# The MLP's inner width in 11 tiles of 126 units, and its weights loaded by runs of units

## The chip, the cores and the metric

The kernel runs on one core of a Trainium2 chip. The metric is the device time of one execution in microseconds; the time before is the median of three runs. A profile is one execution recorded by the hardware profiler; lines such as L101 in it are lines of the kernel's file. Engines are named as the profile has them: PE is TensorE (matmuls; PEld is its loading of weights), DVE is VectorE, ACT is ScalarE, POOL is GpSimd, SP is SyncE, whose queue (SPq) issues nearly all DMAs here.

## The reference

The input x has 2048 tokens of 512 features. Two branches work on it, and a gate, one sigmoid per token, mixes them:

```python
g = _sigmoid((x * gate_w).sum(-1, keepdims=True))
a = _A_ref(x, A_wqkv, A_w_phi, A_wo)      # linear attention, 32 heads of 16, with a learned softmax feature map
h = jnp.einsum("bsd,df->bsf", x, w1) + b1  # B: 512 -> 1376
act = h * jnp.tanh(softplus(h))            # Mish
b = jnp.einsum("bsf,fd->bsd", act, w2)     # 1376 -> 512
return g * a + (1 - g) * b
```

The change is in branch B, the MLP with an inner width of 1376 units. The gate's weight vector rides along as one more column of w1, so that 1377 units go through the first product.

## The kernel before, in words

Every large product is made of three matmuls in a reduced 4-byte type (F32R): each operand is split into a high part (a copy by ScalarE, `hi`, `wh`, `xh`) and a low part (a subtraction by GpSimd or VectorE, `lo`, `wl`, `xl`), and high x high, high x low and low x high are summed in PSUM. Four small groups stay in plain 4-byte floats: `warm` (filler at the start), `fuse`, `kvp` and `num`, and the transpose `kvT`.

**Stage A** walks over 8 chunks of 256 tokens (c = 0 to 7). For each it makes k, v and q for two groups of 128 tokens (12 matmuls of 512 columns each: `proj`), the feature map of k (`mx`, `mn`, `d0`, `d1` on VectorE, E = exp on ScalarE, the sum `S`, its reciprocal `rS` and the scaling `ml` on VectorE), and sums k's features with v (`kv`, the tile kvp) for two chunks at a time, at the end of each odd chunk up to chunk 5. q goes to DRAM (`st`, the tile pqd) for later. PSUM has three buffers that k and q (and later `up`) take in turn, four that v takes, and one for kvp. So the second k of a chunk takes the buffer that the first q of the chunk before has left, and that buffer is free once ScalarE has copied that q out (`qe`, the tile qs).

Beside this, stage A brings in the MLP's weights. w1 and w2 come in pieces of up to 1024 columns into two raw buffers (`ldw`, two pieces a chunk): w1 in chunks 0 to 2, w2 in chunks 3 to 5. One chunk later ScalarE makes the high part (`wh`) and GpSimd the low part (`wl`); the raw buffer is then free for the next piece. The orders in which the engines get these steps are written out by hand (FIRST, EVEN, ODD, NEXT, LAST, lines 39 to 58), and `pin` keeps each engine to its order. In EVEN and ODD, ScalarE gets in each chunk xh, wh0, E0, wh1, E1, ve0, ve1 (copies of v), qe0, qe1; SP gets ldx (the x of two chunks on), ldw0, ldw1, st0, st1.

**Stage B** walks over 4 blocks of 512 tokens. For each block and each of NF = 11 tiles of the inner width, `up` makes a tile of units by 512 tokens (12 matmuls: 3 products x 4 slices of the 512 features; the weights are the stationary operand, 128 units wide, and the 512 tokens move), `mi` applies Mish with the bias b1s, `hi` and `lo` split it, and `down` multiplies it with w2 for four groups of 128 tokens (3 matmuls each; here the activations are the stationary operand, units by 128 tokens, and the 512 outputs move). The attention's second half (`lq`, `num`, `wo`) goes between them. The last block's last group takes its last two tiles in `rest`, in two halves of 256 columns. The orders are BLOCK0, BLOCK1 and BLOCK.

In the version before, the 1377 units lie in two arrays: w1a (6 tiles of 128, of which the last holds 96 units, the gate's column as its 97th and zeros) and w1b (5 tiles of 128). Every tile is 128 wide. ORDER takes the tile with the gate first, so that `gr` can read the gate's row (GROW, row 96) from the first tile. b1 comes as one DMA of 128 x 11 on GpSimd's queue (L187). A piece of w1 or w2 is one DMA of 128 rows on SP's queue (`piece`, L160).

Of the kernel before, what the change touches and what calls it, by code (L numbers as in the profile page):

```python
# [9 lines left out]
F32 = mybir.dt.float32  # L10
F32R = mybir.dt.float32r
AF = mybir.ActivationFunctionType
# [3 lines left out]
P = 128  # L16
# [4 lines left out]
KT = D // P  # L21
# [5 lines left out]
FA = 736  # L27
NFA = 6
FB = 640
NFB = 5  # L30
NF = NFA + NFB
GROW = FA % P
ORDER = [NFA - 1] + list(range(NFA - 1)) + list(range(NFA, NF))
WARM = 10


# [53 lines left out]
def tile_gated_mix(ctx: ExitStack, tc: tile.TileContext, xT, wv, wkT, wqT, bd, w1a, w1b, b1, w2a, w2b, wo, out):  # L90
# [6 lines left out]
    pin = tc.keep_in_program_order  # L97
    V, G_, A_, Sy = nc.vector, nc.gpsimd, nc.scalar, nc.sync

    def mm(*a, **k):  # L100
        return pin(nc.tensor.matmul(*a, **k))  # L101

    def T(shape, dt, tag, bufs, name):
        nm[0] += 1
        return sp.tile(shape, dt, name=f"{name}_{nm[0]}", tag=tag, bufs=bufs)
# [4 lines left out]
    def k4(name, tag, dt=F32):  # L110
        return T([P, 1024], dt, tag, {"E": 4, "tx": 2, "oh": 2, "z": 1}[tag], name)

    def k2(name, tag, dt=F32):
        return T([P, 512], dt, tag, {"pq": 3, "io": 4, "hl": 8}[tag], name)

    def psum(name, tag, bufs={"a": 3, "dn": 4, "kv": 1}):
        nm[0] += 1
        return pp.tile([P, 512], F32, name=f"{name}_{nm[0]}", tag=tag, bufs=bufs[tag])

    def act(out_, in_, fn=AF.Copy, **k):  # L120
        return pin(A_.activation(out_, in_, fn, **k))  # L121
# [7 lines left out]
    def f32(ap):  # L129
        return ap.bitcast(F32)  # L130
# [3 lines left out]


    def stage(wT):
        return T([P, NFA * 512], F32, "w1a", 2, "wT")[:, : KT * 512].rearrange("p (k g f) -> p k g f", k=KT, f=P)

    skT, sqT = stage(wkT), stage(wqT)
    bds = k2("bds", "io")[:, :].rearrange("p (g f) -> p g f", g=NG)  # L140
# [17 lines left out]
    def piece(dram, o, n=1024):  # L158
        r = k4("raw", "oh")
        pin(Sy.dma_start(r[:, :n], dram[:, o : o + n]))  # L160
        return r[:, :n]
# [22 lines left out]
    pin(G_.affine_select(md, md, pattern=[[-DH, 8], [0, DH]], compare_op=ALU.is_ge, fill=0.0, base=0, channel_multiplier=1))  # L184
    pin(G_.affine_select(md, md, pattern=[[DH, 8], [0, DH]], compare_op=ALU.is_ge, fill=0.0, base=DH - 1, channel_multiplier=-1))
    b1s = const.tile([P, NF], F32, name="b1s")
    pin(G_.dma_start(b1s, b1))  # L187
    ident = const.tile([P, P], F32, name="ident")
    make_identity(nc, ident)
    mask = const.tile([P, 2, 2, 32], F32, name="mask")  # L190
# [10 lines left out]
    def at(key, name, fn):  # L201
        steps.setdefault((key, name), []).append(fn)
# [143 lines left out]
            at(key, "ldx", lambda: ldx(c + 2))  # L346


    W = {}
    for n_, f in (("w1a", NFA), ("w1b", NFB), ("w2a", NFA), ("w2b", NFB)):  # L350
        W[n_] = None, f * 512
    raws = {}
    PIECES = [(n_, dram, o) for n_, dram in (("w1a", w1a), ("w1b", w1b), ("w2a", w2a), ("w2b", w2b)) for o in range(0, W[n_][1], 1024)]

    def w_ops(c):

        for j, (n_, dram, o) in enumerate(PIECES[2 * c : 2 * c + 2]):
            cs = slice(o, min(o + 1024, W[n_][1]))

            def ld(n_=n_, dram=dram, cs=cs):  # L360
                raws[n_, cs.start] = piece(dram, cs.start, cs.stop - cs.start)

            def wh(n_=n_, cs=cs):
                hl, n = W[n_]
                if hl is None:
                    hl = [T([P, n], F32R, n_, 2, n_ + x) for x in "hl"]
                    W[n_] = hl, n
                act(hl[0][:, cs], raws[n_, cs.start])

            def wl(n_=n_, cs=cs):  # L370
                h, l = W[n_][0]
                pin(G_.tensor_sub(l[:, cs], raws[n_, cs.start], f32(h[:, cs])))

            at(("A", c), f"ldw{j}", ld)
            at(("A", c + 1), f"wh{j}", wh)
            at(("A", c + 1), f"wl{j}", wl)

    def w1_tile(f, x, k):
        n_, f, n = ("w1a", f, NFA) if f < NFA else ("w1b", f - NFA, NFB)
        return W[n_][0][x][:, (k * n + f) * P : (k * n + f + 1) * P]  # L380

    def w2_tile(f, x):
        n_, f = ("w2a", f) if f < NFA else ("w2b", f - NFA)
        return W[n_][0][x][:, f * 512 : (f + 1) * 512]


    xb = {}
# [86 lines left out]
    def b_ops(b):  # L474
        key = ("B", b)
        U, dn, tts, eTs, num, ohl, io = {}, {}, {}, {}, {}, {}, {}

        def up(i):
            f = ORDER[i]
            xh, xl = xb[b]  # L480
            ps = psum("up", "a")
            n = 0
            for w, a in ((0, xh), (1, xh), (0, xl)):
                for k in range(KT):
                    mm(ps, w1_tile(f, w, k), a[:, k, :], start=(n == 0), stop=(n == 3 * KT - 1))
                    n += 1
            U[i] = {"ps": ps}

        def mi(i):
            f = ORDER[i]  # L490
            U[i]["a"] = k2("act", "hl")
            act(U[i]["a"], U[i]["ps"], AF.Mish, bias=b1s[:, f : f + 1])

        def hi(i):
            U[i]["h"] = k2("h", "hl", F32R)
            act(U[i]["h"], U[i]["a"])

        def lo(i):
            U[i]["l"] = k2("l", "hl", F32R)
            pin(G_.tensor_sub(U[i]["l"], U[i]["a"], f32(U[i]["h"])))  # L500

        last_t = 3 if b == NB - 1 else None

        def down(i, t):
            if t not in dn:
                dn[t] = psum("down", "dn")
            f = ORDER[i]
            h, l = [U[i][x][:, t * P : (t + 1) * P] for x in "hl"]
            for n, (a, x) in enumerate(((h, 0), (h, 1), (l, 0))):
                mm(dn[t], a, w2_tile(f, x), start=(i == 0 and n == 0), stop=(i == (NF - 3 if t == last_t else NF - 1) and n == 2))  # L510

        for i in range(NF):
            at(key, f"up{i}", lambda i=i: up(i))
# [3 lines left out]
            for t in range(4):  # L517
                if t != last_t or i < NF - 2:
                    at(key, f"dn{i}" if i < NF - (2 if b == NB - 1 else 1) else f"df{t}", lambda i=i, t=t: down(i, t))


        cs = slice(4 * b, 4 * b + 4)
# [95 lines left out]
        for t in range(4):  # L618
            def wo_(t=t):
                num["wo", t] = ps = psum("wo", ("kv", "a")[t % 2])  # L620
                woh, wol = [kt(wob[x], 512) for x in "hl"]
                n = 0
                for G in range(NG):
                    o = (G % 2) * SC + (t % 2) * P
                    hl = ohl[t // 2, G // 2]
                    h, l = hl[:, o : o + P], hl[:, 512 + o : 512 + o + P]
                    for a, w in ((h, woh), (h, wol), (l, woh)):
                        mm(ps, a, w[:, G, :], start=(n == 0), stop=(n == 3 * NG - 1))
                        n += 1

            def ag(t=t):
                i = 4 * b + t
                io[t] = k2("io", "io")
                act(io[t], num["wo", t], scale=g_sb[:, i : i + 1])

            def most():

                i = S // P - 1
                pin(V.scalar_tensor_tensor(io[3], dn[3], og_sb[:, i : i + 1], io[3], op0=ALU.mult, op1=ALU.add))

            def rest():

                i = S // P - 1
                for j, eng in enumerate((Sy, A_)):
                    cs = slice(256 * j, 256 * j + 256)
                    ps = psum("rest", "a")[:, :256]
                    n = 0
                    for u in (NF - 2, NF - 1):
                        h, l = [U[u][x][:, 3 * P :] for x in "hl"]
                        for a, x in ((h, 0), (h, 1), (l, 0)):  # L650
                            mm(ps, a, w2_tile(ORDER[u], x)[:, cs], start=(n == 0), stop=(n == 5))
                            n += 1
                    pin(V.scalar_tensor_tensor(io[3][:, cs], ps, og_sb[:, i : i + 1], io[3][:, cs], op0=ALU.mult, op1=ALU.add))  # L653
                    pin(eng.dma_start(out[i * P : (i + 1) * P, cs], io[3][:, cs]))

            def fi(t=t):
                i = 4 * b + t
                pin(V.scalar_tensor_tensor(io[t], dn[t], og_sb[:, i : i + 1], io[t], op0=ALU.mult, op1=ALU.add))
                pin(Sy.dma_start(out[i * P : (i + 1) * P, :], io[t]))

            at(key, f"wo{t}", wo_)
            at(key, f"ag{t}", ag)
            if t == last_t:
# [51 lines left out]
    for j in range(2):  # L715
        h, l = [w[:, 2 * j : 2 * j + 2, :].rearrange("p k f -> p (k f)") for w in (wvh, wvl)]
# [14 lines left out]
    for i in range(4):  # L731
        wh, wl = [halves(w, slice(i // 2 * 2, i // 2 * 2 + 2))[i % 2] for w in (wqh, wql)]
# [77 lines left out]
```

## Time and profile before

| what | value |
|---|---|
| median of 3 runs | 451.03 us (450.79 to 451.19) |
| profiled execution | 451.0 us |
| its span, first to last instruction | 449.3 us |
| instructions in it | 7222 |
| TensorE clock granted, mean | 0.999 |
| DMA | 40.09 MB, mean 89 GB/s |

The profile's parts are the busy time of each engine as a share of the span, the chain of work that ended last (followed back from the last instruction, each step to what released it), groups of equal instructions with their mean time, and the DMA queues. A row of a timeline or chain begins with its start and its length in us; a group of n instructions in a row ends in xn. A window of the DMA view lists packets by size.

### The profile page before, as it was taken

How to read it: one execution, taken by the hardware profiler on the slowest of the kernel's cores; microseconds unless marked ns; L12 is line 12 of the kernel's file. 1: busy time of each engine (PE TensorE's matmuls, PEld its weight loads, DVE VectorE, ACT ScalarE, POOL GpSimd, SP SyncE). 2: the span in 40 equal slices, each digit the busy share in tenths (PEclk: the TensorE clock that was granted, in tenths of full speed). 3: DMA queues.
4: the chain of work that ended last, by engine and by line, in shares of the span. 5: the costliest groups of instructions: out<-in, count | busy, mean ns of one | idle time of the engine just before them, and what ended most of it. 6: DMA issues, size and time to landing. Idle time of an engine off the chain costs nothing.

```text
span 449.3 us, 7222 instructions
## 1 busy us (share of the span) xinstructions
PE 443.9 (99%) x2886; PEld 362.8 (81%) x2886; DVE 306.0 (68%) x408; ACT 195.0 (43%) x269; POOL 163.0 (36%) x102
## 2 busy tenths in 40 slices
PE   8999999999999999999999999999999999999997
PEld 7888888888888888878787887887887888787885
DVE  2798558459399999997979976476967529611003
ACT  3644533444325555627355453534253543244221
POOL 3448687677862345621122212014212122221211
PEclk9999999999999999999999999999999999999999
DMA  7721522514523111405143151331151302030002
GB/s 272 268 95 47 190 69 95 190 15 172 189 84 106 48 24 25 117 19 154 64 125 111 39 148 48 82 107 47 36 149 47 86 13 95 1 82 13 1 0 95
DMA packets 25883, 40.09 MB, mean 89 GB/s; under 512 B 5749, under 2 KB 14197, under 8 KB 25849
## 3 DMA queue, kind: packets, MB, share of 16 engines
q1 hardware_dynamic: 25528, 39.22, 28.6%
q8 instruction: 23, 0.38, 0.3%
q10 hardware_dynamic: 288, 0.39, 0.3%
q14 instruction: 12, 0.09, 0.1%
q0 software_dynamic: 32, 0.01, 0.0%
HBM read 22.82 MB, written 8.40 MB: 69 GB/s over the span
## 4 chain that ended last, share of the span: by engine, by line
PE 98%; DMA 1%; ACT 0%; DVE 0%; issue 0%
PE proj L101 29%; PE up L101 27%; PE down L101 26%; PE wo L101 10%; PE num L101 2%; PE kvp L101 2%; DMA bds<-in_bd_dram 1%; PE fuse L101 1%; PE rest L101 0%; PE z L101 0%; ACT wkh L121 0%; PE warm L101 0%; DVE io L653 0%; PE kvT L456 0%
## 5 line engine op out<-in xcount | busy, mean ns | idle before, releaser
L500 POOL TENSOR_TENSOR l<-act,h 128x512 fp32r<-128x512 f32 x44 | 63.2, 1438 | 221.9 <-ACT h L121 183.6
L121 ACT ACTIVATE act<-up,b1s 128x512 f32<-128x512 f32 x44 | 30.3, 688 | 89.0 <-PE up L101 88.8
L320 POOL TENSOR_TENSOR zacc<-zacc,E 128x1024 f32<-128x1024 f32 x16 | 39.7, 2483 | 42.7 <-DVE E L282 32.6
L121 ACT ACTIVATE E<-E 128x1024 f32<-128x1024 f32 x32 | 33.6, 1059 | 47.3 <-DVE E L267 44.3
L282 DVE TENSOR_TENSOR E<-E,Sm 128x1024 f32<-128x1024 f32 x32 | 45.7, 1427 | 1.1
L271 DVE TENSOR_REDUCE Sm<-E 128x64 f32<-128x1024 f32 x32 | 38.7, 1210 | 5.0 <-ACT E L121 5.0
L101 PE MATMUL wo<-woh,ohl 128*128 128x512 f32 x128 | 40.7, 389 | 0.0
L101 PE MATMUL down<-w2ah,h 128*128 128x512 f32 x96 | 37.5, 390 | 0.0
L101 PE MATMUL down<-w2al,h 128*128 128x512 f32 x96 | 37.4, 390 | 0.0
L101 PE MATMUL down<-w2ah,l 128*128 128x512 f32 x96 | 37.4, 389 | 0.0
L258 DVE TENSOR_REDUCE mx<-proj 128x32 f32<-128x512 f32 x16 | 11.0, 690 | 30.7 <-PE proj L101 30.7
L101 PE MATMUL down<-w2bh,h 128*128 128x512 f32 x78 | 30.5, 391 | 0.0
L101 PE MATMUL down<-w2bl,h 128*128 128x512 f32 x78 | 30.4, 390 | 0.0
L101 PE MATMUL down<-w2bh,l 128*128 128x512 f32 x78 | 30.4, 389 | 0.0
L121 ACT ACT_TABLE_LOAD x19 | 24.4, 1283 | 10.1 <-PE up L101 9.8
L121 ACT ACTIVATE h<-act 128x512 fp32r<-128x512 f32 x44 | 27.8, 632 | 1.4
L612 DVE TENSOR_TENSOR ohl<-num,ohl 128x512 fp32r<-128x512 f32 x16 | 10.3, 683 | 26.5 <-ACT ohl L121 26.3
L101 PEld LDWEIGHTS wo<-woh,ohl 128*128 128x128 f32 x128 | 24.0, 188 | 5.0
L101 PE MATMUL up<-xbh,w1ah 128*128 128x512 f32 x96 | 26.2, 395 | 0.0
L101 PE MATMUL up<-xbh,w1al 128*128 128x512 f32 x96 | 25.7, 390 | 0.0
L101 PE MATMUL up<-xbl,w1ah 128*128 128x512 f32 x96 | 25.7, 390 | 0.0
L405 DVE TENSOR_TENSOR xbl<-xraw,xbh 128x1024 fp32r<-128x1024 f32 x8 | 12.2, 1562 | 19.8 <-ACT xbh L121 19.8
(121 smaller groups left out, 966.6 us busy)
## 6 DMA issues: line engine op xcount, KB each, us to landing
eT<-tt SPq DMA_DIRECT2D x128, 64.0 KB, 2.0
xraw<-in_xT_dram SPq DMA_DIRECT2D x15, 512.0 KB, 4.4
pqd<-qs SPq DMA_DIRECT2D x16, 256.0 KB, 3.1
pq<-pqd SPq DMA_DIRECT2D x16, 256.0 KB, 2.9
out_dram<-io SPq DMA_DIRECT2D x15, 256.0 KB, 2.1
raw<-in_w1a_dram SPq DMA_DIRECT2D x3, 512.0 KB, 4.3
raw<-in_w2a_dram SPq DMA_DIRECT2D x3, 512.0 KB, 4.0
wT<-in_wkT_dram SPq DMA_DIRECT2D x4, 256.0 KB, 5.2
```

The lines of the kernel that those rows point to most:

```text
L101: return pin(nc.tensor.matmul(*a, **k))
L121: return pin(A_.activation(out_, in_, fn, **k))
L258: pin(V.tensor_reduce(d[name], hv(src()), axis=AX.X, op=op))
L271: pin(V.tensor_reduce(d["S"], hv(d["E"][:, :]), axis=AX.X, op=ALU.add))
L282: pin(eng.tensor_mul(hv(d["E"][:, :]), hv(d["E"][:, :]), d["S"][:, :, None].to_broadcast([P, 2 * H, DH])))
L320: at(key, f"z{t}", lambda d=d: pin(G_.tensor_add(zacc, zacc, d["E"])))
L405: pin(V.tensor_sub(xb[b][1][:, :, sl], kt(raw[h], SC), f32(xb[b][0][:, :, sl])))
L500: pin(G_.tensor_sub(U[i]["l"], U[i]["a"], f32(U[i]["h"])))
L612: pin(V.tensor_sub(ohl[h, gp][:, 512:], num[h, gp], f32(ohl[h, gp][:, :512])))
```

## The change

The 1377 units are put in one row: first the 97 of the tile with the gate, then w1a's first 640, then w1b's 640 (RUNS). This row is cut into 11 tiles of 126 units, the last of 117. `size(i)` is the width of tile i, and `runs(o, n)` says which stretches of the arrays in DRAM units o to o + n are. The arrays in DRAM are as before.

- w1 becomes one pair of arrays of 4 x 1377 columns in SBUF (before: two pairs, with 4 x 768 and 4 x 640). Its pieces are six, as before, and each is filled by one to four DMAs of 128 rows, one for each run of columns, 17 in all.
- A tile of w2 now holds rows of up to two stretches of DRAM that lie on other partitions than in SBUF. Each stretch is loaded by one DMA of so many rows of 2 KB, 21 in all, and its units' b1 by another DMA of as many rows of one element, on the same queue. The numbers of rows by tile are: 97 and 29; 99 and 27; 101 and 25; 103 and 23; 105 and 21; 107 and 19; 109 and 17; 111 and 15; 113 and 13; 115 and 11; 117. The pieces are as before, two tiles each, the last with one.
- `up` has weights of 126 (117) columns, `mi`, `hi`, `lo`, `wh` and `wl` of w2 work on 126 (117) partitions, and `down` and `rest` multiply over 126 (117) rows.
- The orders by hand, the number of matmuls and their order are as before; ORDER goes, since the tile with the gate comes first in the row.

```diff
-NF = NFA + NFB
-GROW = FA % P
-ORDER = [NFA - 1] + list(range(NFA - 1)) + list(range(NFA, NF))
+RUNS = (("a", 640, FA - 640 + 1), ("a", 0, 640), ("b", 0, FB))
+GROW = FA - 640
+NU = FA + 1 + FB
+FT = 126
+NF = -(-NU // FT)
...
-    pin(G_.dma_start(b1s, b1))
...
+    def runs(o, n):
+        r, z = [], 0
+        for part, u, m in RUNS:
+            a, e = max(o, z), min(o + n, z + m)
+            if a < e:
+                r.append((part, u + a - z, e - a, a - o))
+            z += m
+        return r
+
+    def size(i):
+        return min(FT, NU - i * FT)
+
+    W = {"w1": (None, KT * NU), "w2a": (None, NFA * 512), "w2b": (None, NFB * 512)}
...
+    def ld_w1(r, o, n):
+        for k in range(KT):
+            a, e = max(o, k * NU), min(o + n, (k + 1) * NU)
+            for part, u, m, z in runs(a - k * NU, e - a) if a < e else ():
+                src, f = (w1a, NFA * P) if part == "a" else (w1b, FB)
+                pin(Sy.dma_start(r[:, a - o + z : a - o + z + m], src[:, k * f + u : k * f + u + m]))
+
+    def ld_w2(r, i):
+        for part, u, m, z in runs(i * FT, size(i)):
+            while m:
+                j, p = divmod(u, P)
+                c = min(m, P - p)
+                pin(Sy.dma_start(r[z : z + c, :], (w2a if part == "a" else w2b)[p : p + c, j * 512 : (j + 1) * 512]))
+                j += 0 if part == "a" else NFA
+                pin(Sy.dma_start(b1s[z : z + c, i : i + 1], b1[p : p + c, j : j + 1]))
+                u, m, z = u + c, m - c, z + c
...
-            def ld(n_=n_, dram=dram, cs=cs):
-                raws[n_, cs.start] = piece(dram, cs.start, cs.stop - cs.start)
+            def ld(n_=n_, o=o, n=n, tiles=tiles):
+                raws[n_, o] = k4("raw", "oh")
+                if n_ == "w1":
+                    ld_w1(raws[n_, o], o, n)
+                for i, z in tiles:
+                    ld_w2(raws[n_, o][:, z : z + 512], i)
...
-                act(hl[0][:, cs], raws[n_, cs.start])
+                act(hl[0][:rows, cs], raws[n_, cs.start][:rows, :n])
...
-                pin(G_.tensor_sub(l[:, cs], raws[n_, cs.start], f32(h[:, cs])))
+                pin(G_.tensor_sub(l[:rows, cs], raws[n_, cs.start][:rows, :n], f32(h[:rows, cs])))
...
-    def w1_tile(f, x, k):
-        n_, f, n = ("w1a", f, NFA) if f < NFA else ("w1b", f - NFA, NFB)
-        return W[n_][0][x][:, (k * n + f) * P : (k * n + f + 1) * P]
+    def w1_tile(i, x, k):
+        o = k * NU + i * FT
+        return W["w1"][0][x][:, o : o + size(i)]
...
-            ps = psum("up", "a")
+            ps = psum("up", "a")[: size(i), :]
...
-            act(U[i]["a"], U[i]["ps"], AF.Mish, bias=b1s[:, f : f + 1])
+            act(U[i]["a"], U[i]["ps"], AF.Mish, bias=b1s[: size(i), i : i + 1])
```

More of the change, by code (lines that the diff above doesn't have):

```diff
@@ L136, in stage @@
     def stage(wT):
-        return T([P, NFA * 512], F32, "w1a", 2, "wT")[:, : KT * 512].rearrange("p (k g f) -> p k g f", k=KT, f=P)
+        return T([P, KT * NU], F32, "w1", 2, "wT")[:, : KT * 512].rearrange("p (k g f) -> p k g f", k=KT, f=P)
     skT, sqT = stage(wkT), stage(wqT)
@@ L346, in a_ops @@
             at(key, "ldx", lambda: ldx(c + 2))
-    W = {}
-    for n_, f in (("w1a", NFA), ("w1b", NFB), ("w2a", NFA), ("w2b", NFB)):
-        W[n_] = None, f * 512
-    raws = {}
-    PIECES = [(n_, dram, o) for n_, dram in (("w1a", w1a), ("w1b", w1b), ("w2a", w2a), ("w2b", w2b)) for o in range(0, W[n_][1], 1024)]
+    def runs(o, n):
[6 more added lines that the diff above has]
+        return r
@@ new lines, in size @@
+    def size(i):
+        return min(FT, NU - i * FT)
+    W = {"w1": (None, KT * NU), "w2a": (None, NFA * 512), "w2b": (None, NFB * 512)}
+    raws = {}
+    PIECES = [(n_, o) for n_, (_, f) in W.items() for o in range(0, f, 1024)]
+    def ld_w1(r, o, n):
[4 more added lines that the diff above has]
+                pin(Sy.dma_start(r[:, a - o + z : a - o + z + m], src[:, k * f + u : k * f + u + m]))
@@ L355, in w_ops @@
+    def ld_w2(r, i):
[7 more added lines that the diff above has]
+                u, m, z = u + c, m - c, z + c
     def w_ops(c):
-        for j, (n_, dram, o) in enumerate(PIECES[2 * c : 2 * c + 2]):
+        for j, (n_, o) in enumerate(PIECES[2 * c : 2 * c + 2]):
@@ L358, in w_ops @@
             cs = slice(o, min(o + 1024, W[n_][1]))
-            def ld(n_=n_, dram=dram, cs=cs):
-                raws[n_, cs.start] = piece(dram, cs.start, cs.stop - cs.start)
-            def wh(n_=n_, cs=cs):
-                hl, n = W[n_]
+            n = cs.stop - o
+            tiles = [] if n_ == "w1" else [(o // 512 + (NFA if n_ == "w2b" else 0) + t, t * 512) for t in range(n // 512)]
+            rows = min([size(i) for i, _ in tiles], default=P)
+            def ld(n_=n_, o=o, n=n, tiles=tiles):
[4 more added lines that the diff above has]
+                    ld_w2(raws[n_, o][:, z : z + 512], i)
@@ L365, in wh, with wl @@
+            def wh(n_=n_, cs=cs, n=n, rows=rows):
+                hl, m = W[n_]
                 if hl is None:
-                    hl = [T([P, n], F32R, n_, 2, n_ + x) for x in "hl"]
-                    W[n_] = hl, n
-                act(hl[0][:, cs], raws[n_, cs.start])
-            def wl(n_=n_, cs=cs):
+                    hl = [T([P, m], F32R, n_, 2, n_ + x) for x in "hl"]
+                    W[n_] = hl, m
+                act(hl[0][:rows, cs], raws[n_, cs.start][:rows, :n])
+            def wl(n_=n_, cs=cs, n=n, rows=rows):
@@ L376, in w_ops, with w2_tile @@
             at(("A", c + 1), f"wl{j}", wl)
-    def w1_tile(f, x, k):
-        n_, f, n = ("w1a", f, NFA) if f < NFA else ("w1b", f - NFA, NFB)
-        return W[n_][0][x][:, (k * n + f) * P : (k * n + f + 1) * P]
-    def w2_tile(f, x):
-        n_, f = ("w2a", f) if f < NFA else ("w2b", f - NFA)
-        return W[n_][0][x][:, f * 512 : (f + 1) * 512]
+    def w1_tile(i, x, k):
+        o = k * NU + i * FT
+        return W["w1"][0][x][:, o : o + size(i)]
+    def w2_tile(i, x):
+        n_, j = ("w2a", i) if i < NFA else ("w2b", i - NFA)
+        return W[n_][0][x][: size(i), j * 512 : (j + 1) * 512]
     xb = {}
@@ L478, in up @@
         def up(i):
-            f = ORDER[i]
             xh, xl = xb[b]
-            ps = psum("up", "a")
+            ps = psum("up", "a")[: size(i), :]
             n = 0
@@ L484, in up @@
                 for k in range(KT):
-                    mm(ps, w1_tile(f, w, k), a[:, k, :], start=(n == 0), stop=(n == 3 * KT - 1))
+                    mm(ps, w1_tile(i, w, k), a[:, k, :], start=(n == 0), stop=(n == 3 * KT - 1))
                     n += 1
@@ L489, in mi @@
         def mi(i):
-            f = ORDER[i]
-            U[i]["a"] = k2("act", "hl")
-            act(U[i]["a"], U[i]["ps"], AF.Mish, bias=b1s[:, f : f + 1])
+            U[i]["a"] = k2("act", "hl")[: size(i), :]
+            act(U[i]["a"], U[i]["ps"], AF.Mish, bias=b1s[: size(i), i : i + 1])
         def hi(i):
-            U[i]["h"] = k2("h", "hl", F32R)
+            U[i]["h"] = k2("h", "hl", F32R)[: size(i), :]
             act(U[i]["h"], U[i]["a"])
         def lo(i):
-            U[i]["l"] = k2("l", "hl", F32R)
+            U[i]["l"] = k2("l", "hl", F32R)[: size(i), :]
             pin(G_.tensor_sub(U[i]["l"], U[i]["a"], f32(U[i]["h"])))
@@ L506, in down @@
                 dn[t] = psum("down", "dn")
-            f = ORDER[i]
             h, l = [U[i][x][:, t * P : (t + 1) * P] for x in "hl"]
             for n, (a, x) in enumerate(((h, 0), (h, 1), (l, 0))):
-                mm(dn[t], a, w2_tile(f, x), start=(i == 0 and n == 0), stop=(i == (NF - 3 if t == last_t else NF - 1) and n == 2))
+                mm(dn[t], a, w2_tile(i, x), start=(i == 0 and n == 0), stop=(i == (NF - 3 if t == last_t else NF - 1) and n == 2))
         for i in range(NF):
@@ L650, in rest @@
                         for a, x in ((h, 0), (h, 1), (l, 0)):
-                            mm(ps, a, w2_tile(ORDER[u], x)[:, cs], start=(n == 0), stop=(n == 5))
+                            mm(ps, a, w2_tile(u, x)[:, cs], start=(n == 0), stop=(n == 5))
                             n += 1
```

## The prediction, made before the changed kernel ran

> **What bounds the kernel now.** I read the page first: its busy shares, then the chain of work that ended last.
>
> ```profile
> span 449.3 us, 7222 instructions
> PE 443.9 (99%) x2886; PEld 362.8 (81%) x2886; DVE 306.0 (68%) x408; ACT 195.0 (43%) x269; POOL 163.0 (36%) x102
> PE 98%; DMA 1%; ACT 0%; DVE 0%; issue 0%
> ```
>
> TensorE's matmuls are busy 99% of the span and make 98% of the chain: no other engine, queue or transfer is late anywhere now, so only what makes a matmul longer, or makes one wait, changes the time. The profiled execution took 451.0 us, 1.7 us more than its span; the median of the three runs is 451.03 us, so sums made on the profiled one carry over as they stand.
>
> The chain in order of time gives the price of single matmuls (columns: start us, us, engine, group, matmuls):
>
> ```profile
> 6.71 0.64 PE warm L101 x4
> ...
> 114.39 1.92 PE kvp L101 x128
> ...
> 163.47 2.72 PE up L101 x12
> 166.19 0.44 PE kvT L456 x4
> ...
> 444.58 1.44 PE rest L101 x12
> ```
>
> up: 12 matmuls moving 512 columns in 2.72 us, 226.7 ns each. rest: same kind, 256 columns, 1.44/12 = 120.0 ns. The slope is 106.7/256 = 0.4167 ns a column, so 512 columns cost 213.3 ns and 13.3 ns are left over whatever the width: the part of the weight load that shows. 13.3 ns is 32 column times for 128 weight columns, four at a time. In the two plain 4-byte groups much more shows: kvT, 128 columns through a 128-column load, takes 110 ns, 56.7 above its 53.3; warm takes 160 ns, which is three times 53.3, two for moving and one for the load. There a load goes one column at a time.
>
> **Part 1: narrower weight tiles in up.** The order on TensorE is the same, 2886 matmuls. down and rest keep 128 weight columns (the tokens) and have 126 or 117 rows in them. up's weight tile has 126 columns (117 in the last of 11 tiles). The cost of such a load is in no row. From below: 13.3 ns, the nearest row by type; a saving is excluded but for 2/128 of it. From above: kvT's 56.7 ns times 126/128, 55.8. I take the upper kind, because 13.3 ns is a quarter of 128 columns and 126 has no four equal quarters, and price it at the array's own pace: 126 x 0.4167 = 52.5 ns, for 117 columns 48.8. up runs 4 blocks x 11 tiles x 12 = 528 matmuls, 480 wide and 48 narrow: 480 x 39.2 + 48 x 35.4 ns = **20.5 us** (22.2 at kvT's price), all on the path, since up's matmuls stand in the chain back to back. A tile of 12 goes from 2.72 to 3.19 us.
>
> The Trainium skill ("TensorE: Matmul & The Clock Gate", "Weight-path perf modes — Fast Weight Load (FWL) and DoubleRow") says that the fast load is on when the number of weights is 128 and the type isn't FP32. By it the sum stands as I have it. The same page ("LDWEIGHTS (loading the stationary operand)") gives columns / 1.2 ns; by that an estimate is 105 ns a load, and the sum would be 48 us.
>
> **Part 2: w2 and b1 in runs of units.** A piece of w2 was one DMA of 128 rows; now each of its tiles is one or two runs of units, and each run two DMAs on SP's queue: rows of 2 KB and a column of b1, 4 bytes a row. SP's queue grows by 47 instructions. How many transfer engines does such a DMA use? Each engine ends its share with a small packet, so packets under 512 B count engines. Three windows: one piece of w2a, 128 rows (71.0 to 75.2 us, whose 40 slices also show when bytes begin, 71.9); the single row gd<-gr (158.6 to 159.9); and pq, rows of 2 KB at full load (162.1 to 162.6).
>
> ```profile
> GB/s 0 0 0 0 0 0 0 0 0 156 195 195 78 195 351 312 273 273 273 234 312 351 546 390 273 390 78 39 78 0 0 0 0 0 0 0 0 0 0 0
> DMA packets 144, 0.52 MB, mean 125 GB/s; under 512 B 16, under 2 KB 16, under 8 KB 144
> ```
> ```profile
> DMA packets 2, 0.00 MB, mean 2 GB/s; under 512 B 1, under 2 KB 1, under 8 KB 2
> ```
> ```profile
> DMA packets 92, 0.19 MB, mean 373 GB/s; under 512 B 1, under 2 KB 1, under 8 KB 92
> ...
> q1 hardware_dynamic: 92, 0.19, 98.0%
> ```
>
> 128 rows went to 16 engines in equal shares, one row to one. Runs here have 97, 101, 103, 107, 109, 113 rows: primes, which have no equal shares but one. The bounds: 16 engines (no cost: as many bytes as before) or one. I take equal shares, on the same first engines each time, the pattern of both rows. In the third window, 0.5 us, 16 engines x 0.5 x 98% = 7.84 us of engine time carried 91 rows: 86 ns a row of 2 KB on one engine. The 4-byte element is priced by ge_sb<-gd, 512 of them (160.9 to 161.8):
>
> ```profile
> DMA packets 535, 0.02 MB, mean 18 GB/s; under 512 B 528, under 2 KB 528, under 8 KB 535
> ```
>
> That window is 0.9 us long, 32 elements an engine: at most 28 ns each, at least nothing beside other work. Halfway, 14, makes 100 ns a row, bounds 86 and 114. With shares by the largest divisor up to 16, the first engine gets these rows of each piece: A (tiles 0, 1) 97+29+9+3 = 138; B (2, 3) 101+5+103+23 = 232; C (4, 5) 7+3+107+19 = 136; D (6, 7) 109+17+37+1 = 164; E (8, 9) 113+1+23+1 = 138; F 9. B alone is 23.2 us of one engine, and a stage-A chunk is 16.4 us.
>
> The Trainium skill ("DMA: Bandwidth & Descriptors", "Why a DMA increments its semaphore by 16 and not by 1") says that a DMA takes the largest number up to 16 dividing its slowest dimension, the lowest-numbered engines on SP's queue, and one engine for 127 partitions. No run here shows that yet; by it the sum stands.
>
> Who waits? ScalarE converts each piece in order, ahead of E, v and qs of the same chunk. Rows of SP, ScalarE, GpSimd, VectorE and TensorE, in that order:
>
> ```profile
> 71.07 8.30 SPq L160 DMA_DIRECT2D raw<-in_w2a_dram  x2
> ```
> ```profile
> 81.22 1.05 ACT L121 ACTIVATE w2ah<-raw 128x1024 fp32r<-128x1024 f32 x1
> 87.10 1.06 ACT L121 ACTIVATE E<-E 128x1024 f32<-128x1024 f32 x1 [4.83 <-DVE E L267]
> 88.07 1.04 ACT L121 ACTIVATE w2ah<-raw 128x1024 fp32r<-128x1024 f32 x1
> 89.83 1.06 ACT L121 ACTIVATE E<-E 128x1024 f32<-128x1024 f32 x1 [0.71 <-DVE E L267]
> 90.79 0.58 ACT L121 ACTIVATE v<-proj 128x512 f32<-128x512 f32 x1
> 92.67 0.60 ACT L121 ACTIVATE v<-proj 128x512 f32<-128x512 f32 x1 [1.29 <-PE proj L101]
> 95.44 0.60 ACT L121 ACTIVATE qs<-proj 128x512 f32<-128x512 f32 x1 [2.17 <-PE proj L101]
> ```
> ```profile
> 103.42 2.43 POOL L372 TENSOR_TENSOR w2al<-raw,w2ah 128x1024 fp32r<-128x1024 f32 x1
> ```
> ```profile
> 108.92 1.21 DVE L271 TENSOR_REDUCE Sm<-E 128x64 f32<-128x1024 f32 x1
> 110.17 0.55 DVE L279 RECIPROCAL Sm<-Sm 128x64 f32<-128x64 f32 x1
> 110.76 1.90 DVE L282 TENSOR_TENSOR E<-E,Sm 128x1024 f32<-128x1024 f32 x1
> ```
> ```profile
> 100.63 1.07 PE L101 MATMUL proj<-wkh,xh 128*128 128x512 f32 x4
> ...
> 135.41 1.07 PE L101 MATMUL proj<-wkh,xh 128*128 128x512 f32 x4
> ```
>
> A is issued at 71.07 and moves from 72.0 to 85.8 (before, to 74.0 by the slices); its conversion slips from 81.2 to 86, which E at 87.10 still covers: nothing. B ends at 109.0, and its conversion, due at 88.07, ends at 110.0; behind it E, two v and the first qs end at 112.9. The second k of chunk 5 needs the PSUM buffer of that qs: it starts at 112.9 instead of 100.63. C follows two stores of qs and the next x, 2.7 us of each engine (64 KB of each engine's share at 373/16 GB/s):
>
> ```profile
> xraw<-in_xT_dram SPq DMA_DIRECT2D x15, 512.0 KB, 4.4
> pqd<-qs SPq DMA_DIRECT2D x16, 256.0 KB, 3.1
> ```
>
> C runs from 111.7 to 125.3, D to 141.7 (GpSimd has freed its buffers in time: B's low part, 2.43 us, ends by 114). D's conversion, E and the three VectorE steps add 5.8: chunk 5's kv can start at 147.5. TensorE has run out of other work at 127.5 (112.9 + 5 groups of 2.72 + chunk 4's kv) and waits 20 us. kv of chunk 5 is the second half of the kvp row, due at 115.35: **32.1 us** late. In one line: 72.0 + 670 rows x 100 ns + 2.7 + 5.8 - 115.35; with 86 ns it is 22.8, with 114 ns 41.5. E lands at 158.2 and its followers on ScalarE free their PSUM buffer by 164; TensorE wants it for chunk 7's second k, at 135.41 + 32.1 = 167.5, so nothing is added, and F is 9 rows.
>
> **Part 3: the restart.** After the idle start TensorE was slow for a while:
>
> ```profile
> 1.12 4.21 PE L101 MATMUL warm<-ones 128*128 128x128 f32 x20 [1.12 <-DVE ones L170]
> ```
>
> 20 matmuls took 4.21 us that take 3.2 at warm's later pace: 1.0 us lost. Two long waits: **2.0 us**, between 0 and 4.
>
> **Parts at nothing.** w1 as one array: 17 DMAs of 128 rows for 6, all in equal shares of 16. At SP's 0.33 us each they delay a piece by at most 1.0 us:
>
> ```profile
> 38.46 0.33 SPq L160 DMA_DIRECT2D raw<-in_w1a_dram  x1
> ```
> ```profile
> 46.44 1.05 ACT L121 ACTIVATE w1ah<-raw 128x1024 fp32r<-128x1024 f32 x1
> ```
> ```profile
> raw<-in_w1a_dram SPq DMA_DIRECT2D x3, 512.0 KB, 4.3
> ```
>
> It lands at 42.8 and is used at 46.44: 3.7 us cover it; without the cover it costs 1 us. Mish, h and l work on 126 partitions with the same 512 elements each, beside TensorE. b1's old DMA on POOL goes from a queue that nobody waits for. What is late next, after part 1, is TensorE itself.
>
> **Sum:** 451.0 + 20.5 + 32.1 + 2.0 = **505.6 us**; within this case 494 (451.0 + 20.5 + 22.8) to 519 (451.0 + 22.2 + 41.5 + 4).
>
> **Rivals.** (1) Only the transfers cost: the load of 126 columns keeps its 13.3 ns, or a longer one hides behind the 213 ns of the matmul ahead. For it: the load unit's 81% is below the matmuls' 99%. Against: 13.3 ns shows in every row of this type, and full loads in kvT and warm. 451.0 + 34.1 = 485.1. The same page of the Trainium skill ("Step-by-step: what each phase is for") says that loads are pulled ahead of matmuls in flight; by that it would be this case. (2) Only the loads cost: uneven runs are dealt over 16 engines, or each onto another engine. Then the longest run, 115 rows, is 11.5 us, and a piece has 17 us from issue (71.07) to use (88.07). 471.5. (3) down loses too, because its weights have 126 rows: 522 + 12 loads x 40 ns (53.3 - 13.3) = 21.4 more: 527.0. (4) Not slower: load and shares both stay as in the rows of before; TensorE moves the same columns in the same order, and the narrower load saves at most 0.2 ns x 528 = 0.1 us. It decides where a 126-column load shows under 14 ns and no run of w2 takes over 17 us. 451.0.
>
> **Chances.** Forecast 0.62, (1) 0.14, (2) 0.13, (3) 0.05, (4) 0.06. The range leaves out (3) and (4) and has to take in (2): 471 to 519. A measurement of this kernel tells about 0.2% from no change. Case (4) gives same 0.05 and faster 0.01; slower by over 0.2% gets 0.94.
>
> **What would show it.** up x12 at 3.19 us in the chain with down still at 2.72 (part 1; 2.72 refutes it, down at 3.2 is rival 3). raw<-in_w2a landing after 10 us or more, ScalarE's w2 conversions waiting for DMA, TensorE idle some 12 us before the second k of chunk 5 and some 20 us before its kv (part 2; landings near 4 us refute it). w1 pieces landing near 4 us (covered). I am most easily wrong in the 4-byte elements' price and in the chain of waits behind B and D.

## The result, and the profile after

The changed kernel took **482.69 us** (median of 5 runs, 482.06 to 483.12) against 451.03 us before (5 runs, 450.79 to 451.19): 1.0702 times as long, 95% interval 1.0689 to 1.0715. It is slower, inside the predicted range, but 23 us faster than the forecast of 505.6. The time is closest to rival (1), "only the transfers cost", at 485.1. The profiled execution took 483.1 us.

The page of the changed kernel, its busy shares, two rows of its 40 slices and its chain:

```profile
span 481.4 us, 7299 instructions
PE 453.3 (94%) x2886; PEld 365.2 (76%) x2886; DVE 304.6 (63%) x408; ACT 194.1 (40%) x269; POOL 160.9 (33%) x101
PE   8999999939439999999999999999999999999997
PEclk9999999988859999999999999999999999999999
PE 76%; SPq 12%; DVE 6%; DMA 2%; issue 2%; POOL 1%; ACT 1%; POOLq 0%; ACTq 0%
```

TensorE was busy all along before; now it has a hole in the slices that run from about 96 to 144 us, the granted clock (PEclk) sags there, and SP's queue stands in the chain with 12%. From about 150 us on all is full again. So I split the time at the first up, which ends stage A. First the rows before the change (the first is the first k of chunk 6, used further down), then the one after:

```profile
116.24 1.20 PE L101 MATMUL proj<-wkh,xh 128*128 128x512 f32 x4
...
151.39 1.20 PE L101 MATMUL up<-xbh,w1ah 128*128 128x512 f32 x4
```
```profile
179.45 1.19 PE L104 MATMUL up<-xbh,w1h 128*126 128x512 f32 x4
```

Stage A grew by 28.1 us. The rest of the span was 449.3 - 151.4 = 297.9 and is 481.4 - 179.5 = 301.9: stage B grew by 4.0. Together 32.1, the growth of the span.

**Where stage A lost it.** ScalarE's timeline in the changed kernel, its conversions of the pieces B, C and D of w2, with the idle time ahead of each and what ended it:

```profile
105.93 1.06 ACT L124 ACTIVATE w2ah<-raw 126x1024 fp32r<-126x1024 f32 x1 [17.55 <-DMA raw<-in_w2a_dram]
106.89 1.04 ACT L124 ACTIVATE E<-E 128x1024 f32<-128x1024 f32 x1
120.51 1.06 ACT L124 ACTIVATE w2ah<-raw 126x1024 fp32r<-126x1024 f32 x1 [9.47 <-DMA raw<-in_w2b_dram]
121.47 1.04 ACT L124 ACTIVATE E<-E 128x1024 f32<-128x1024 f32 x1
136.11 1.06 ACT L124 ACTIVATE w2bh<-raw 126x1024 fp32r<-126x1024 f32 x1 [13.59 <-DMA raw<-in_w2b_dram]
137.07 1.04 ACT L124 ACTIVATE E<-E 128x1024 f32<-128x1024 f32 x1
```

TensorE's timeline beside it: the second k of chunk 5 waits for a qs, and the kv of chunk 5 for v and E, all of which stand behind those conversions on ScalarE:

```profile
109.45 2.07 PE L104 MATMUL proj<-wkh,xh 128*128 128x512 f32 x4 [8.44 <-ACT qs L124]
111.32 1.57 PE L104 MATMUL proj<-wkl,xh 128*128 128x512 f32 x4
112.72 1.07 PE L104 MATMUL proj<-wkh,xl 128*128 128x512 f32 x4
...
138.65 1.08 PE L104 MATMUL kvp<-E,v 128*32 128x64 f32 x32 [12.95 <-ACT v L124]
141.35 1.08 PE L104 MATMUL kvp<-E,v 128*32 128x64 f32 x32 [1.62 <-DVE E L284]
142.37 2.08 PE L104 MATMUL proj<-wkh,xh 128*128 128x512 f32 x4
144.24 1.91 PE L104 MATMUL proj<-wkl,xh 128*128 128x512 f32 x4
145.95 1.35 PE L104 MATMUL proj<-wkh,xl 128*128 128x512 f32 x4
147.14 1.08 PE L104 MATMUL proj<-wkh,xh 128*128 128x512 f32 x4
```

These are the two waits of the prediction, at the same two instructions and by the same chain, each somewhat shorter. The first row after each wait also shows the slow restart: a group of four takes 2.07 us where it settles at 1.07. The granted clock goes with it: it was 0.50 from 138.6 to 146.0 us, 0.88 from 146.0 to 148.1 and 1.00 from there to the end of stage A.

**How many engines carried a run?** Two windows of the DMA view, 88 to 104 us and 110 to 130 us, in which nearly only runs of w2 and b1 move:

```profile
GB/s 26 26 26 26 26 20 26 26 26 41 87 51 16 1 21 21 26 5 26 26 26 26 26 26 26 26 26 26 26 26 26 26 20 26 26 26 26 1 11 26
DMA packets 440, 0.40 MB, mean 25 GB/s; under 512 B 243, under 2 KB 243, under 8 KB 440
...
q1 hardware_dynamic: 440, 0.40, 7.5%
```
```profile
DMA packets 482, 0.48 MB, mean 24 GB/s; under 512 B 254, under 2 KB 254, under 8 KB 481
...
q1 hardware_dynamic: 481, 0.47, 6.9%
```

The shares are taken over 16 engines, so one busy engine is 1/16 = 6.25%: 7.5 and 6.9% say that there was little more than one at work, at 26 GB/s in most slices, where the 128-row piece of before had reached 546. The small packets can't count engines here, since most of them are b1's elements; the share can.

**Stage B**, first a down of the kernel before (its up stands in the prediction, 2.72), then the chain of the changed kernel:

```profile
160.75 2.72 PE down L101 x12
```
```profile
186.69 2.79 PE up L104 x12
189.47 2.74 PE down L104 x12
```

up went from 2.72 to 2.79 us, not to the predicted 3.19. down is at 2.74. Each has about 44 such groups of 12 (4 blocks x 11 tiles): 44 x 0.07 = 3.1 us for up and 44 x 0.02 = 0.9 us for down make the 4.0.

### The profile page after: what moved, and what is told of

Same layout as the page of the kernel before. It is cut to its first block, busy times and chain, and to the rows that moved or that the text cites. A ratio compares the mean times of both kernels' runs of the same rounds, so it can differ in the third digit from the quotient of the medians.

```text
span 481.4 us, 7299 instructions
## 1 busy us (share of the span) xinstructions
PE 453.3 (94%) x2886; PEld 365.2 (76%) x2886; DVE 304.6 (63%) x408; ACT 194.1 (40%) x269; POOL 160.9 (33%) x101
## 4 chain that ended last, share of the span: by engine, by line
PE 76%; SPq 12%; DVE 6%; DMA 2%; issue 2%; POOL 1%; ACT 1%; POOLq 0%; ACTq 0%
PE up L104 25%; PE down L104 25%; PE proj L104 12%; PE wo L104 9%; SPq L381 8%; SPq L383 4%; PE num L104 2%; DVE Sm L273 1%; DMA pqd<-qs 1%; DVE E L284 1%; DMA bds<-in_bd_dram 1%; DVE xbl L444 1%; PE fuse L104 1%; DVE E L269 1%; PE kvp L104 1%
## 5 line engine op out<-in xcount | busy, mean ns | idle before, releaser
L537 POOL TENSOR_TENSOR l<-act,h 126x512 fp32r<-126x512 f32 (+1 forms) x44 | 63.9, 1453 | 223.6 <-ACT h L124 153.8
L104 PE MATMUL up<-xbh,w1h 128*126 128x512 f32 (+1 forms) x176 | 48.7, 398 | 0.0
L104 PE MATMUL up<-xbl,w1h 128*126 128x512 f32 (+1 forms) x176 | 48.1, 395 | 0.2 <-DVE xbl L444 0.2
L104 PE MATMUL up<-xbh,w1l 128*126 128x512 f32 (+1 forms) x176 | 48.0, 394 | 0.0
L104 PEld LDWEIGHTS up<-xbh,w1h 128*126 128x126 f32 (+1 forms) x176 | 32.1, 186 | 10.1 <-issue 2.9
L104 PEld LDWEIGHTS up<-xbl,w1h 128*126 128x126 f32 (+1 forms) x176 | 32.6, 186 | 8.9 <-DVE xbl L444 0.6
L104 PEld LDWEIGHTS up<-xbh,w1l 128*126 128x126 f32 (+1 forms) x176 | 32.6, 185 | 8.1
L104 PE MATMUL down<-w2ah,h 126*128 126x512 f32 x96 | 37.6, 391 | 0.0
L104 PE MATMUL down<-w2ah,l 126*128 126x512 f32 x96 | 37.5, 391 | 0.0
L104 PE MATMUL down<-w2al,h 126*128 126x512 f32 x96 | 37.5, 391 | 0.0
```

## The experiments

The theory after the result: a DMA whose number of rows has no divisor but one goes to a single engine, and this is the whole of stage A's 28 us; a 126-column load costs little, since it hides beside the matmul ahead. Runs told as one time were single executions with a profile.

**1. The kernel before, its w2 in runs of 97 and 31 rows** (two primes). Nothing else is changed:

```diff
-                raws[n_, cs.start] = piece(dram, cs.start, cs.stop - cs.start)
...
+                for o in range(0, cs.stop - cs.start, 512):
+                    for p0, p1 in ((0, 97), (97, P)):
+                        pin(Sy.dma_start(r[p0:p1, o : o + 512], dram[p0:p1, cs.start + o : cs.start + o + 512]))
...
```

> The kernel before, tiles of 128 units, but each tile of w2 is loaded by two DMAs, of 97 and of 31 rows of 2 KB (before: one DMA of 128 rows for two tiles). Nothing else changes. Theory (a number of rows that no number up to 16 divides goes to one engine, the same each time): all 256 rows of a piece pass one engine at 86 to 91 ns, 22 to 23 us a piece against chunks of 16.4 us; by the prediction's sum the kv of chunk 5 is 72.0 + 1024 rows x 88 ns + 2.7 + 5.8 - 115.35 = 55 us late, and the next piece adds some 5, restarts some 5: 516 us, 505 to 525. Rival (uneven runs are dealt over all engines, or each to another engine): 451 to 453 us, landings near 4 us.

Measured: 515.37 us (before, beside it: 451.13, 13 runs). ScalarE's waits in it (us in all, times, longest):

```profile
ACT w2ah L121 <- DMA raw<-in_w2a_dram: 49.2, 3, 18.9
ACT w2bh L121 <- DMA raw<-in_w2b_dram: 36.9, 2, 18.8
```

Full 128-unit tiles, no b1 in between, the same bytes: 64 us lost by the row counts alone.

**2. The same with runs of 96 and 32 rows.** The edit is that of run 1 with 96 for 97.

> The same as e1_before_97_31 with runs of 96 and 32 rows: as many DMAs and bytes. Theory (equal shares on 16 engines): 451.0 us, within 0.5, up at 2.72 us a tile. Rival (the cost is in the number of DMAs or in SP's issuing): as slow as with 97 and 31 rows, over 470 us.

Measured: 451.63 us (451.27 to 451.92, 10 runs), 1.0011 times before, interval 1.0002 to 1.0021. The same number of DMAs and one row of difference: half a microsecond. Its DMA view in the window of 71 to 76 us, where four DMAs were issued:

```profile
DMA packets 320, 0.52 MB, mean 105 GB/s; under 512 B 64, under 2 KB 64, under 8 KB 320
...
q1 hardware_dynamic: 320, 0.52, 35.8%
```

64 small packets from four DMAs are 16 engines each, counted as the prediction counted them. So neither the splitting nor SP's longer queue costs more than that; the row counts do. The Trainium skill's rule in "DMA: Bandwidth & Descriptors" ("Why a DMA increments its semaphore by 16 and not by 1"), the largest number up to 16 that divides the rows, agrees with runs 1 and 2 and with the 6.9% above.

**3. The changed kernel with w2 and b1 laid out by tiles in DRAM**, so that each piece is one DMA of 128 rows again; the 126-unit tiles and w1 stay:

```diff
+    pin(G_.dma_start(b1s, b1))
...
-                for i, z in tiles:
-                    ld_w2(raws[n_, o][:, z : z + 512], i)
+                else:
+                    pin(Sy.dma_start(raws[n_, o][:, :n], (w2a if n_ == "w2a" else w2b)[:, o : o + n]))
...
```

> The changed kernel with w2 and b1 laid out in DRAM in its own order of units, so that a piece of w2 is one DMA of 128 rows again and b1 one DMA of 128 x 11 on POOL's queue. up's tiles of 126 and w1's runs stay. Theory (the wait in stage A comes from w2's and b1's runs alone; the rest is up's tiles at 2.79 us for 2.72): 451.0 + 44 x 0.07 + at most 1 = 453.5 to 455.5 us, no wait of TensorE in stage A. Rival (w1's narrow runs or something else of the new layout make the wait): 470 us or more.

Measured: 455.33 us (455.18 to 455.44), 1.0093 times before, 1.0078 to 1.0108. In its timeline the first up starts where it does in the kernel before; in its chain up is as slow as in the changed kernel:

```profile
151.40 1.19 PE L104 MATMUL up<-xbh,w1h 128*126 128x512 f32 x4
```
```profile
158.15 2.79 PE up L104 x12
```

So the loads of w2 and b1 are all of stage A's loss (w1's 17 DMAs cost nothing), and what is left, some 4 us, comes with the new tiles, which are narrower and start at other columns.

**4. The changed kernel with b1 as one DMA on GpSimd's queue again**, laid out by tiles in DRAM, and w2's runs as they are, to part the rows from the 4-byte elements:

```diff
+    pin(G_.dma_start(b1s, b1))
...
-                pin(Sy.dma_start(b1s[z : z + c, i : i + 1], b1[p : p + c, j : j + 1]))
...
```

> The changed kernel with b1 as one DMA of 128 x 11 on POOL's queue again (b1 laid out by tiles in DRAM), so that SP's queue loses the 21 DMAs of single elements; w2's runs stay. Theory A (an element costs about 5 ns on its engine, as the landings of the changed kernel give: 91 ns a row of data and element less 86 for the data): 670 x 5 = 3.5 us less than the changed kernel, 479 us, 476 to 482. Theory B (an element costs 28 ns, ge_sb's pace): 19 us less, 464 us.

Measured: 478.57 us (478.26 to 479.06), 1.0612 times before, 1.0594 to 1.0629. b1's 21 DMAs cost 4.1 of the 28 us; over the 670 elements ahead of the second wait that is 6 ns each, not 14, if all of it goes by the element and none by the DMA. The rows of w2 are the rest. Without b1 the small packets count engines again: in the window of 71 to 84.5 us, in which piece A passes, 22 packets are under 512 B. The runs of A have 97, 29, 99 and 27 rows, and 1 + 1 + 11 + 9 is 22, the equal shares that the prediction counted with.

**5. The price of a narrower load: the kernel before, with up's tiles narrowed in place** to 128, 127, 126, 125, 124, 120, 112, 117, 96, 126 and 128 columns by step. The units cut off are left out of the sum.

```diff
-        return W[n_][0][x][:, (k * n + f) * P : (k * n + f + 1) * P]
+        return W[n_][0][x][:, (k * n + f) * P : (k * n + f) * P + wid]
...
```

> The kernel before with up's weight tiles narrowed in place, at their old start addresses: widths by step 0 to 10 of a block 128, 127, 126, 125, 124, 120, 112, 117, 96, 126, 128 columns; Mish, h, l and the rows of w2 narrow with them, so the units that are cut off are left out of the sum. One look at up's matmuls by width. Theory A (the 5 to 6 ns more of a matmul in the changed kernel come from a load that isn't 128 columns wide): the narrowed steps take 2.78 to 2.80 us, the two of 128 take 2.72. Theory B (they come from where the columns start in SBUF): every step takes 2.72 us, 451 us in all. The prediction's price of a load of single columns, 2.9 us or more for some width, would show only where a width falls out of the fast form.

**6. The kernel before, with up's 128 columns starting 0, 1, 2, 3, 4, 8, 16, 32, 1, 2 and 0 columns further right** by step. The products are then those of the wrong units.

```diff
-        return W[n_][0][x][:, (k * n + f) * P : (k * n + f + 1) * P]
+        return W[n_][0][x][:, (k * n + f) * P + off : (k * n + f + 1) * P + off]
...
```

> The kernel before with up's weight tiles 128 columns wide, but starting 0, 1, 2, 3, 4, 8, 16, 32, 1, 2, 0 columns (of 4 bytes) to the right for steps 0 to 10 of a block, so that shifted steps multiply by the wrong columns. Theory A (width): every step 2.72 us, 451 us in all. Theory B (start address): the steps with offsets that aren't a multiple of 16 columns take 2.78 to 2.80 us, the others 2.72; 453 us in all.

Measured: 454.14 and 453.55 us (before, beside them: 451.0, 7 runs). From the traces, the mean time from one matmul's start to the next inside a tile, without the first two of a tile, in ns, step by step:

```
step               0      1      2      3      4      5      6      7      8      9     10
5: width         128    127    126    125    124    120    112    117     96    126    128
5: ns          226.9  226.7  233.4  231.7  228.3  233.0  230.4  235.8  229.9  233.3  227.9
6: start +         0      1      2      3      4      8     16     32      1      2      0
6: ns          227.0  231.8  230.4  229.2  226.6  233.4  233.4  232.8  232.2  230.8  226.7
```

A width of 126 costs 6.5 ns a matmul, and none costs near the 39.2 of the prediction. 127 columns, with no equal quarters either, cost nothing, which leaves nothing of the quarters. But the small loss isn't one of width alone: 128 columns from another start lose as much, and +4 loses nothing where +8 does. A width or a start that stands in two steps gives the same within 1 ns, so this is hardly noise, though each kernel ran once. Neither theory had it, and **its cause stays open**.

**7. The changed kernel with each run split at its largest multiple of 16**, b1 as one DMA, w2's place in DRAM unchanged:

```diff
-                pin(Sy.dma_start(r[z : z + c, :], (w2a if part == "a" else w2b)[p : p + c, j * 512 : (j + 1) * 512]))
+                for q0, q1 in ((0, c // 16 * 16), (c // 16 * 16, c)):
+                    if q0 < q1:
+                        pin(Sy.dma_start(r[z + q0 : z + q1, :], (w2a if part == "a" else w2b)[p + q0 : p + q1, j * 512 : (j + 1) * 512]))
...
```

> The changed kernel with b1 as one DMA on POOL's queue, and each run of w2 split in two DMAs: the largest multiple of 16 rows, and the rest of under 16 rows. DRAM's w2 stays as it was. Theory (16 equal shares, and a rest of n rows goes to n engines): a piece lands about as fast as before; TensorE doesn't wait in stage A, or under 2 us at SP's 16 issues a piece; 451.0 + 4.3 for up = 455.3 us, 454.5 to 458. Rival (each DMA of the piece has its own price on the way, whatever its rows): with twice as many DMAs as in the kernel with b1 apart, over 478 us.

Measured: 454.70 us (454.38 to 455.03), 1.0079 times before, 1.0062 to 1.0096. More DMAs, and the wait is gone. ScalarE's conversions of A and B in its timeline are back at their old places (81.22 and 88.07 before):

```profile
81.35 1.05 ACT L124 ACTIVATE w2ah<-raw 126x1024 fp32r<-126x1024 f32 x1
88.19 1.04 ACT L124 ACTIVATE w2ah<-raw 126x1024 fp32r<-126x1024 f32 x1
```

Its DMA view in the window of 71 to 76 us, in which the eight DMAs of piece A move:

```profile
DMA packets 345, 0.52 MB, mean 105 GB/s; under 512 B 92, under 2 KB 92, under 8 KB 344
```

92 small packets are four times 16, for the multiples of 16, and 1 + 13 + 3 + 11 for the rests, each rest of n rows on n engines.

Against run 4, the same kernel with the runs whole, it is 23.9 us faster.

**8. Run 3 with w1's arrays enlarged to 4 x 1408 columns**, so that all arrays behind them in SBUF start where 128-unit tiles would put them:

```diff
...
-                    hl = [T([P, m], F32R, n_, 2, n_ + x) for x in "hl"]
+                    hl = [T([P, KT * NF * P if n_ == "w1" else m], F32R, n_, 2, n_ + x) for x in "hl"]
```

> The changed kernel with w2 and b1 whole (as in e3_after_w2_whole), and the two w1 arrays enlarged to 4 x 1408 columns so that the second array and all behind it start where they would with tiles of 128; the tiles inside stay at 1377 columns a slice and 126 a tile. Theory A (width) and theory B (start of each tile) both: no change to 455.3 us, since the tiles' own starts are as uneven as before. Rival (the uneven start of the second array alone): 451 to 452 us.

Measured: 454.78 us (454.67 to 455.48), 1.0086 times before, 1.0071 to 1.0101. The places of the arrays are not what costs the 4 us; the tiles inside w1 still start at the same uneven columns.

**9. Is the load hidden? The kernel before, with wo's matmuls cut along the moving columns**, until they are shorter than their load (in block 3 with narrower weights, which leaves out part of the products):

```diff
+                    m = (512, 256, 128, 128)[b]
+                    part = (128, 112, 96, 80)[t] if b == 3 else 128
...
-                        mm(ps, a, w[:, G, :], start=(n == 0), stop=(n == 3 * NG - 1))
+                        wid = part if n else P
+                        for o in range(0, 512, m):
+                            mm(ps[:wid, o : o + m], a[:, :wid], w[:, G, o : o + m], start=(n == 0), stop=(n == 3 * NG - 1), skip_group_check=True)
```

> The kernel before, with wo's 24 matmuls of a tile cut along the moving columns: block 0 as before (512), block 1 in two of 256, block 2 in four of 128, block 3 in four of 128 with weights 128, 112, 96 and 80 columns wide in its four groups of tokens (in block 3 the narrower groups leave out part of the products, all but the first of the 24). It asks whether the load of the weights shows as a remainder on top of the moving columns (the prediction: 13.3 ns, whatever the width) or lies hidden beside the matmul ahead and bounds only matmuls that are shorter than it. Theory (hidden load, about 0.83 ns a weight column as its records have it, 188 ns being record and not pace): start to start 226.7 ns at 512, 120 at 256, then about 107 to 110 at 128 by 128, and at 128 moving columns 94 to 97 with 112 weight columns, 80 to 83 with 96, 67 to 70 with 80; a tile of wo in block 2 takes about 10.4 us, the span grows by some 33 us to about 482. Rival (the prediction's reading, a load in quarters that shows): 66.7 ns at 128 moving columns in all widths that have four equal quarters; a tile of wo in block 2 takes 6.4 us, the span grows by about 9 us to 458.

Measured: 469.28 us (before, beside it: 450.86). wo in the chain, blocks 0, 1, 2 and 3:

```profile
197.68 5.44 PE wo L101 x24
...
254.58 5.75 PE wo L101 x48
...
328.47 10.67 PE wo L101 x96
...
412.36 10.08 PE wo L101 x96
440.09 7.74 PE wo L101 x96
```

Block 2 moves as many columns as block 0 in twice the time: 111 ns a matmul, where 13.3 on top of 53.3 would be 66.7 (6.4 us for the 96). TensorE's timeline in block 3 gives the other widths:

```profile
418.35 0.95 PE L101 MATMUL wo<-woh,ohl 128*112 128x128 f32 x8
419.14 0.56 PE L101 MATMUL wo<-wol,ohl 128*112 128x128 f32 x4
...
440.66 0.84 PE L101 MATMUL wo<-woh,ohl 128*96 128x128 f32 x8
441.34 0.50 PE L101 MATMUL wo<-wol,ohl 128*96 128x128 f32 x4
...
444.80 0.74 PE L101 MATMUL wo<-woh,ohl 128*80 128x128 f32 x8
445.37 0.45 PE L101 MATMUL wo<-wol,ohl 128*80 128x128 f32 x4
```

Start to start, eight matmuls took 0.79, 0.68 and 0.57 us with 112, 96 and 80 weight columns. The means over all such matmuls in the trace are 111.7 (128 columns, without four gaps of under 60 ns), 98.3, 85.1 and 71.7 ns: 13.3 ns for every 16 columns, 0.83 ns a weight column and 5 ns more. The theory holds and the quarters fall: by this line a 128-column load takes about 107 ns, an estimate, and it lies hidden beside the longer matmuls, since 256 and 512 moving columns stay at 119.8 and 226.7 ns. The rise of the time was 18 us and not 33, because a row of 24 matmuls is wo for two groups of tokens, and my sum had counted it for one. The Trainium skill's columns / 1.2 ns in "TensorE: Matmul & The Clock Gate" ("LDWEIGHTS (loading the stationary operand)") is 0.83 ns a column and agrees. Its section on FWL has a fast load at 128 weights where the type isn't FP32, and no gain for fp32; F32R isn't named there, and here it shows none: 128 columns lie on the same line as 112, 96 and 80.

No kernel here beats the one before; runs 3, 7 and 8 come within 4.2 us of it.

## Why the prediction was right in its direction and wrong in its size

- **What bounds the kernel: right.** TensorE stood in 98% of the chain, and all that was lost came as longer matmuls in stage B (4.0 us) or in stage A as waits of TensorE and the slow matmuls behind them (28.1).
- **Part 1, the narrower loads: wrong, the failed step.** The step was "13.3 ns is a quarter of 128 columns and 126 has no four equal quarters", which made a load of 52.5 ns and 20.5 us. Run 9 shows that a load of 80 to 128 columns takes 0.83 ns a column, is over in 107 ns, and hides behind 213 ns of moving. The 13.3 ns do not go with the load: with 96 weight columns and 512 moving the spacing was 229.9 ns (run 5), no shorter. What they are stays open. kvT's 110 ns, from which the prediction read a full load visible on top, is close to run 9's 111.7 ns for 128 moving columns bounded by a 128-column load; no run varied kvT or warm themselves. The prediction added the load to the moving time, where in run 9 the longer of the two decides. The sum's 20.5 us measured 3.1 (2.79 against 2.72 for up); down, which part 1 left as it was, lost another 0.9. The prediction's rival (1) had just this, and the section of the Trainium skill that it names there, "Step-by-step: what each phase is for", stands in "TensorE: Matmul & The Clock Gate". The load unit's busy share, 81% beside 99%, spoke for it and should have weighed more. What the remaining 6 ns are, runs 5, 6 and 8 don't settle.
- **Part 2, the runs on one engine: right, only the size was off.** Prime rows went to one engine (runs 1 and 2, and the packets of runs 4 and 7), the same two instructions of TensorE waited, by the same chain through ScalarE, A was covered and w1 cost nothing (run 3). kv of chunk 5 is two halves of 32 matmuls, and the sum's chain ends in the second. It was forecast at 147.5 and came at 141.35; before it started at 115.68 (115.35, the prediction's due time, is about where the first half starts). It was 25.7 us late where the sum had 32.1. The term that was mis-sized is the row: from 72.0 to 136.1, less the sum's 2.7 for the stores and x, 670 rows took 61.4 us, 91.6 ns each, not 100. That is the 86 ns for 2 KB and about 6 ns for an element (run 4), not the 14 halfway between the bounds.
- **Part 3, the restart: the size was near, the count wrong.** After the first wait two groups of four took 3.27 us from start to start (109.45 to 112.72) where two of the settled pace take 1.81 (8 x 226.7 ns): 1.5 us lost. After the second wait the slow half of kv took 0.5 longer than before, so that the first k of chunk 6 started 26.1 us late (142.37 against 116.24), and the first up came 28.1 late, another 1.9: 2.4 lost. But only this second loss is on the path, since the first ends inside the second wait, whose end ScalarE sets. The sum counted two losses of 1.0 where one of 2.4 counts.
- **Rival (3), down with 126 rows: refuted.** 2.73 to 2.77 us a group, where 3.2 was its sign.
- **The sum by what was measured:** 451.0 + 4.0 + 25.7 + 2.4 = 483.1, beside the profiled execution's 483.1.

## What to carry to other kernels

Before a tile is cut to an odd size, look at the row counts of the DMAs that this makes: a prime count above 16 puts all on one engine, and splitting it at a multiple of 16 repairs it (478.6 to 454.7 us here) even though there are more DMAs. Read it from a window's share (6.9 and 7.5% here, where one engine of 16 is 6.25%) and not from the number of transfers. And where two durations overlap, price a longer load by whether it passes the matmul that covers it, not by adding it; the test is to shorten the cover until the time stops falling.

## What the runs showed of the hardware that I had not expected

- SP's queue itself is held up by such runs. In the changed kernel its timeline shows the issue of the run behind a prime one taking 6 to 8 us (below, 23 rows behind 103, and 17 behind 109), where a whole piece of 128 rows took 0.33 us before; behind 99, 105 and 111 rows the next run took 0.3 us. The stores of qs, next in the queue, wait behind them. First the kernel before, then the changed one:

```profile
86.24 0.33 SPq L160 DMA_DIRECT2D raw<-in_w2a_dram  x1
```

```profile
94.28 7.41 SPq L381 DMA_DIRECT2D raw<-in_w2a_dram  x1
101.73 1.40 SPq L383 DMA_DIRECT2D b1s<-in_b_dram  x1
103.24 1.21 SPq L312 DMA_DIRECT2D pqd<-qs  x2
...
120.72 7.70 SPq L381 DMA_DIRECT2D raw<-in_w2b_dram  x1
```

- A matmul of 512 columns takes from 226.6 to 235.8 ns start to start with the width and the first column of its weights (runs 5 and 6), with no pattern that I could name.
- After 8.4 and 14.6 us of waiting, TensorE lost 1.5 and 2.4 us before it was back at 1.07 us for four matmuls; the granted clock was 0.50 in the window of 109 to 111 us and again from 138.6 to 146.0.
